# Two scalars by GpSimd's queue, state rows in longer packets, state products copied in halves, and new orders of work

## The chip, the cores and the metric

The kernel runs on one core of one Trainium2 chip. The core has five engines that run side by side, each taking its instructions in its own fixed order: PE (TensorE, matrix products), ACT (ScalarE), DVE (VectorE), POOL (GpSimd) and SP (SyncE). Sixteen DMA engines move data between HBM and the on-chip SBUF; transfers are issued by SP and ACT (hardware queues) and by POOL (the software queue, which can also convert fp32 to fp16 on the way). Matrix products land in PSUM, and only ACT and DVE copy them out. The metric is device time in microseconds (us) of one launch.

## The reference, cut to what matters

```python
B, H, S, Ns, D = 8, 8, 512, 32, 64          # x: (8,8,512,64)  state: (8,8,32,64)
scores = scale * x @ state^T                 # per batch and head, 512 x 32
a      = softmax(scores);   xread = a @ state        # (8,8,512,64)
scores2 = scale * state @ x^T                # 32 x 512
a2     = softmax(scores2);  sread = a2 @ x           # (8,8,32,64)
x = concat([xread, sread], axis=2)           # (8,8,544,64) -> 4352 tokens x 512
h = x @ w_in                                 # 4352 x 2048
g = s * relu(h)**2 + b                       # s and b are two single numbers
out = g @ w_out                              # 4352 x 512
```

## The kernel before, in words

**What it computes, and by which names.** A batch b has 512 x-tokens and 32 state rows for each of 8 heads. `T` is the product of state and x (128 rows: four heads by 32 states, twice), `E` its exponential, `D` the sum over the states, and `a4` the quotient, worked out on ACT as `Ln` and `Exp` of D with a multiplication on DVE. The kernel never forms xread: it multiplies each state by the weights first, `M(b, c)` = state times chunk c of `w_in` (`part_M`, 8 small multiplications, "the state product"), has ACT or DVE copy it from PSUM to SBUF as fp16 (`att_M`), and then multiplies `M` by `a4` (`layer1`, named `h` here; two groups g = 0, 1 of heads are added up). ACT applies relu, DVE squares, and `layer2_first` (batch 0) or `layer2` (all others, with seven products in place of eight from sums of blocks `pd` and of weights `u`) multiplies by `w_out`. s and b come in at the end: `bias_bc` is b times the column sums of `w_out`, and every result is `s * o + bias`.

**How the data come in.** `w_in` is loaded in four chunks `wi[0..3]` (512 columns each), `w_out` in four chunks `wo[0..3]`, and x for each batch as `xn[b]`, all by POOL's queue, which turns fp32 into fp16; each of these lands 512 KB in SBUF. Batch 0's x comes by SP's queue in four parts in fp32 (`x0_load`), and ACT and DVE convert them (`x0_cast`). The states come as `stf[0]` (batch 0, by ACT's queue), `stf[1]` (batches 1 and 2, by POOL's queue) and, later, the rest by SP's queue. `att_st` converts a state and writes it twice side by side (`st16`), PE transposes it, and DVE copies the transposed form to `stT`, which every `T` and `M` reads. POOL's first own instruction is a small copy `gate` that waits for the identity matrix (loaded first on ACT's queue); all of POOL's loads wait behind it. The two single numbers are loaded by SP to four partitions each (`small_load`, L530) and spread to all partitions by a 32x32 transpose on DVE (`spread`, L539).

**What sets the order.** The body calls `op(...)` for each piece of work, which numbers it (0 to 1209). `TURNS` (L17) holds for each engine the list of these numbers in the order in which it runs them, written out by hand. `Plan.order` (L149) walks the lists, keeps a model of times, gives out the buffers (three PSUM pairs `ps`, two single banks `o`, and so on) and, in the first 20 us of its model, puts filler multiplications on `warm` into PE's stream where the model has PE idle. A filler is fixed once the kernel is built: it runs even if PE has other work. A number such as `dma=("sw", MB)` or `lands=` is only an entry of that model.

By the lists, POOL issues: gate, wi0, stf[1], x of batch 1, wi1, wo0, wi2, wo1, wi3, wo2, wo3, x of batch 2. PE runs, in the first 20 us: transposes of x of batch 0, T, D, M(0,0), the transposes of stf[1], h of chunk 0 mixed with the transposes of x of batch 1, M(1,0), M(0,1), T of batch 1, h of chunk 1, and then the first products with wo0.

Of the kernel before, what the change touches and what calls it, by code (L numbers as in the profile page):

```python
# [18 lines left out]
        27 29 25 31 35 33 39 36 40 50 48 80-81 187 84-85 185 53 59 189 92-93 88-89 117 192 118 125-126 121  # L19
        113 122-123 127 119 68 70 114-115 124 116 128 193 120 96 141 129-130 99 237 131-133 225 74 134 142  # L20
        135 145 136 234 137 146 102 147 105 149 148 150-152 161-162 76 108 165-166 240 163 138 111 143
        167-168 164 243 139 222 144 72 62 157 140 158 153 159 56 228 154 160 231 173 155 174 1051 65 330 175
        156 169-171 267 333 258 334 259 268 260-263 269-270 172 176 271 264 272-274 348 351 1056 78 265 345
        354 360 286 277 287-289 694 445 278-281 290-291 282-284 339 357 292 342 293 295-299 454 567 1061
        305-306 300-301 307 302 308 696 576 452 309 315 310 316 311 317 312 318-322 570 572 1066 375-379 448
        689 450 384-387 380 476 388 381-382 467 479 464 389-390 394 482 395 461 391 470 396-397 403 398-401
        473 592 404-405 412 406-407 413-415 408-409 416 410 589 417-419 422 698 692 574 432-436 583 437
        423-424 438 425 439 426-428 586 429 604 601 506 497 507 711 595 498-499 508 598 509 500 510 501-504
        511-512 714 513 516-519 1071 1076 525-526 520-521 527 522-523 528 939 811 529-530 534 531-532
        535-541 544 820 932 935 554-556 545 557-561 546 720 723 619-621 726 622 547-549 705 550-551 623-626  # L30
        717 708 628-630 638-639 631-633 640 634-635 641-642 848 647 643 648-653 644-645 654 845 656-663 1086
        1081 937 941 666-668 676-677 669-670 814 816 818 671-672 678-680 673 954 681 836 741-744 682-683 830
        745-746 957 747 750 748 751-753 833 754-755 760 756 761-763 757 764-766 842 769-770 767 771-775
        778-781 776 782-785 839 788 798-799 789 800 790 801 827 969 963 791 802-805 951 960 1106 792 863 948
        864 793 865 794 866 795 867 1101 868-870 872-878 1091 882 879 883 966 884-888 891-892 1096 889
        893-898 900-906 910 907 911-915 920-921 916-917 1121 1111 984 922 1116 985-986 923 987 924-926
        988-989 927 990 1126 993 991 994-1000 1003-1010 1012-1019 1021-1028 1031-1035 1041 1036 1042
        1037-1038 1043-1048 1143-1150 1152-1159 1162-1169 1171-1178 1180-1187 1190-1197 1200-1207
    """,
    "ACT": """  # L40
        20-21 30 23 37 41 38 42 44 52 45 51 82 86 60 190-191 94 90 194-195 69 197-198 97 100 238 226 235 103
        106 77 109 241 244 223 63 57 229 232 67 331-332 335-336 349 352 79 346 361 355 695 447 446 340 358
# [4 lines left out]
    """,  # L47
    "DVE": """
        24 28 22 26 34 32 6 47 43 49 46 188 83 186 61 7 87 54-55 1057 91 71 95 196 199 98 75 1052 214 101
        239 210 104 215 206 236 107 207 227 110 252 112 218 209 179 177 64 73 245 58 219 242 224 1053 233 66  # L50
        220 230 246 216 253 325 337 183 208 181 247 1058 211 266 248 275 249 347 255 250 256-257 350 356 212
        217 213 285 221 1062 353 254 251 1067 294 341 457 1063 458 303 459 344 369 313 323 1068 363 370 364
        362 359 366 579 371 367 580 365 383 372 581 368 373 392 466 701 402 374 472 1072 484 463 478 469 411
        702 420 481 1077 485 703 475 491 440 585 430 494 594 488 495 492 489 486 588 487 606-608 713 505 597
        514 603 1078 496 493 616 524 940 490 533 1073 542 591 1082 610 936 562 823-824 600 825 944 552 613
        627 1087 617 722 611 945 614 719 636 609 946 728 716 646 615 612 655 707 618 1088 664 1083 942 725
        735 819 710 674 729 684 738 732-733 956 749 730 850 736 739 737 847 758 835 731 768 777 786 734 832
        838 854 740 841 860-861 844 971 959 806 829 855 857 1110 796 851 965 858 852 859 871 962 1105 880
        953 975 856 950 853 972 890 968 1108 899 1103 908 862 976-977 918 1100 981 1098 978 1118 973 1113
        982 928 983 992 979 1125 974 1001 1093 1120 980 1011 1128 1130 1095 1131 1020 1134 1123 1115 1135  # L60
        1029 1137 1140 1136 1138 1132 1141 1039 1049 1151 1160 1133 1142 1170 1139 1179 1188 1198 1208
    """,
    "POOL": """
        8-9 11 16 10 12-15 17-19 329 200 204 202 444 566 180 304 314 276 393 688 810 1060 421 441 182 431
        515 563 324 184 665 178 637 675 1065 1055 759 1070 1080 543 1075 1090 1085 807 685 909 881 919 553
        787 929 797
    """,
    "SP": """
        0-5 327 201 203 328 442 205 443 326 564 338 565 456 1059 687 686 578 460 1064 700 582 1054 704 930
        808-809 931 1079 822 943 1074 826 947 1084 1069 1089 1050 1040 1030 1161 1002 1189 1199 1209  # L70
# [16 lines left out]
class Plan:  # L87
# [60 lines left out]
    def order(self, fill):  # L148
# [3 lines left out]
        dma_free = {"sw": 7.05, "hw": 0.0}  # L152
# [144 lines left out]
def kernel(  # L297
# [88 lines left out]
    few = sb("few", [2], FP32)  # L386
    s32 = sb("s32", [32], FP32)
    b32 = sb("b32", [32], FP32)
    s_bc, b_bc = s32[:, 0:1], b32[:, 0:1]
# [4 lines left out]

    nc.vector.memset(warm, 0.0)
    nc.vector.memset(few, 0.0)
# [9 lines left out]
    for _ in range(4):  # L406
        mm(ob[1], warm[:, 0:P], warm)
    nc.scalar.dma_start(ident16, ident_dr.ap())
    nc.scalar.dma_start(stf[0], st_v[:, 0:NG, :])
# [29 lines left out]
    def x0_load(i):  # L439
        op(  # L440
            {"SP": 0.5},
            lambda e: nc.sync.dma_start(xf_ap(i), x0_v[:, x0_heads(i)]),
            wr=[K(("xf", i))],
            dma=("hw", 0.75),
            lands=(3.6, 4.7, 6.0, 6.5)[i],
        )
# [25 lines left out]
    def wi_load(c):  # L472
        op(
            {"POOL": 0.85},
            lambda e: nc.gpsimd.dma_start(
                out=wi[c],
                in_=moe_w_in.rearrange("(k p) f -> p k f", p=P)[:, :, c * FC : c * FC + FC],
            ),
            rd=[g0],
            wr=[K(("wi", c))],  # L480
            dma=("sw", MB),
        )
# [44 lines left out]
    def small_load(i, src):  # L527
        op(
            {"SP": 0.5},
            lambda e: nc.sync.dma_start(out=few[::32, i : i + 1], in_=src.to_broadcast((4, 1))),  # L530
            wr=[K(("few", i))],
            dma=("hw", 0.1),
            lands=9.8,
        )

    def spread(i, dst, name):
        op(
            {"DVE": 0.12},
            lambda e: nc.vector.transpose(dst, few[:, i : i + 1].to_broadcast((P, 32))),  # L539
            rd=[K(("few", i))],  # L540
            wr=[K((name,))],
        )

    for i in range(4):
        x0_load(i)
    small_load(0, moe_s)
    small_load(1, moe_b)
    spread(0, s32, "s")
    spread(1, b32, "b")
    op(  # L550
# [24 lines left out]
    def att_st(i):  # L575
# [31 lines left out]
        if i == 2:  # L607
# [15 lines left out]
            lambda e: copy(e, stT[:, b0 * NG : b1 * NG], view()[:, 0:n]),  # L623
# [210 lines left out]
    def att_M(b, c, engs=("ACT", "DVE")):  # L834
# [11 lines left out]
        if b == 0 and c < 2:  # L846
            for g in range(NG):
                op(
                    {"ACT": 0.48, "DVE": 0.64},
                    lambda e, g=g: copy(e, T(M[b, c])[:, g], T(u)[:, g]),  # L850
                    rd=[K(u)],
                    wr=[K(M[b, c], g)],
                )
            return
        op(
            {e: {"ACT": 0.92, "DVE": 1.15}[e] for e in engs},
            lambda e: copy(e, T(M[b, c]), T(u)),
            rd=[K(u)],
            wr=[K(M[b, c], g) for g in range(NG)],
        )  # L860

    def att_turn(b, late=False):
        if late:
            after(
                lambda: T(aT[b])[:, 0, 0, 0:2],
# [553 lines left out]
```

## Time and profile before

| | |
|---|---|
| three runs | 207.46, 208.20, 208.53 us; median 208.2 |
| the profiled execution | 208.01 us, of which the profile's span is 206.2 |
| PE busy (fillers included) | 199.3 us, 97% of the span |
| DVE, ACT, POOL busy | 164.3, 109.3 and 38.8 us |
| TensorE clock granted | 1.0 |
| read from HBM, written to it | 17.33 MB, 8.91 MB |

The page is made from one execution. The span runs from the first instruction to the last; the 1.8 us between it and the execution's own time lie around it. Lines of the matrix products all read L335, since one helper issues them, so they are told apart by their operands: `pair<-wi,stT` is M, `pair<-a,M` is h, `o<-wo,g` is layer 2 of batch 0, `o<-warm` or `pair<-warm` is a filler. `stf` in a row stands for either part of the states, `L422` is the helper for copies.

### The profile page before, as it was taken

The numbers are of one execution on the slowest core, as the hardware profiler recorded it, in microseconds if no ns is written. First come the engines' busy times: TensorE is split into PE (matmuls) and PEld (weight loads), VectorE is DVE, ScalarE is ACT, GpSimd is POOL, SyncE is SP. The second block draws the span as 40 slices with busy tenths as digits, with TensorE's granted clock in tenths as the row PEclk, the third lists the DMA queues.
The fourth block names the chain that finished last, engine by engine and source line by source line (L and its number), as shares of the span: only waits on it lengthen the run. The fifth ranks groups of instructions, "written<-read, shape, count | busy, mean of one in ns | idle before, by whom it ended". The sixth has DMA issues, their size and how long they took to land.

```text
span 206.2 us, 4768 instructions
## 1 busy us (share of the span) xinstructions
PE 199.3 (97%) x1989; PEld 134.7 (65%) x1989; DVE 164.3 (80%) x325; ACT 109.3 (53%) x153; POOL 38.8 (19%) x60
## 2 busy tenths in 40 slices
PE   7979999999999999999999999999999999999992
PEld 3744444435666665677577767766776688888881
DVE  2327637989899979899999988997969689859871
ACT  4757786467588879468644473254606634130000
POOL 4832002001020120331301030033070200331000
PEclk9999999999999999999999999999999999999999
DMA  5999999992999992798991470233020200253054
GB/s 173 201 197 204 206 205 179 179 198 16 186 139 195 143 221 41 110 134 154 199 194 60 80 222 13 51 111 118 0 103 3 102 0 2 71 187 105 0 176 131
DMA packets 47285, 25.83 MB, mean 125 GB/s; under 512 B 31616, under 2 KB 45440, under 8 KB 47264
## 3 DMA queue, kind: packets, MB, share of 16 engines
q0 software_dynamic: 13792, 15.34, 38.0%
q1 hardware_dynamic: 33056, 10.10, 26.4%
q8 instruction: 15, 0.25, 0.5%
q10 hardware_dynamic: 416, 0.10, 0.2%
q14 instruction: 6, 0.05, 0.1%
HBM read 17.33 MB, written 8.91 MB: 127 GB/s over the span
## 4 chain that ended last, share of the span: by engine, by line
PE 89%; DMA 7%; DVE 1%; issue 0%; ACT 0%; POOL 0%; DVEq 0%
PE o L335 48%; PE pair L335 41%; DMA wi<-in_moe_w_in_dram 4%; DMA out_dram<-osb 2%; DMA ident<-ident_const 1%; DVE osb L1281 0%; DVE M L422 0%; ACT M L422 0%; DVE osb L1270 0%; DVE aN L906 0%; DVE sr L933 0%; POOL gate L552 0%; DVEq L1270 0%
## 5 line engine op out<-in xcount | busy, mean ns | idle before, releaser
L996 ACT ACTIVATE g<-pair 128x1024 f16<-128x1024 f32 x64 | 63.0, 1023 | 44.5 <-PE pair L335 44.4
L335 PE MATMUL pair<-a,M 128*128 128x512 f16 x256 | 63.3, 379 | 0.1
L335 PEld LDWEIGHTS <-pd 128*128 128x128 f16 x480 | 46.4, 98 | 10.1 <-issue 1.5
L335 PEld LDWEIGHTS <-g 128*128 128x128 f16 x424 | 40.7, 98 | 17.5 <-issue 2.9
L1002 DVE TENSOR_TENSOR g<-g 128x1024 f16<-128x1024 f16 x64 | 42.8, 683 | 2.8 <-ACT g L996 2.8
L335 PE MATMUL o<-u,pd 128*128 128x256 f16 x360 | 44.2, 273 | 0.0
L335 PE MATMUL o<-wo,g 128*128 128x256 f16 (+1 forms) x272 | 42.6, 285 | 0.0
L335 PEld LDWEIGHTS <-M 128*128 128x128 f16 x256 | 24.7, 98 | 22.9 <-DVE M L422 0.6
L1173 POOL DMA_DIRECT2D out_dram<-osb x28 | 18.8, 724 | 103.2 <-DVE osb L1281 54.5
L1270 DVE SCALAR_TENSOR_TENSOR osb<-o,s,bias_bc 128x512 f32<-128x512 f32 (+1 forms) x32 | 22.9, 715 | 7.3 <-PE o L335 5.7
L422 ACT CAST M<-pair 128x1024 f16<-128x1024 f32 (+1 forms) x22 | 20.4, 958 | 7.8 <-PE pair L335 7.8
L1281 DVE SCALAR_TENSOR_TENSOR osb<-o,s,osb 128x512 f32<-128x512 f32 (+1 forms) x24 | 17.2, 716 | 7.6 <-PE o L335 7.4
L1082 DVE TENSOR_TENSOR pd<-g 128x1024 f16<-128x1024 f16 (+1 forms) x32 | 20.7, 651 | 0.1
L335 PE MATMUL o<-wo,pd 128*128 128x256 f16 x120 | 19.0, 273 | 0.0
L335 PE MATMUL o<-u,g 128*128 128x256 f16 x120 | 17.5, 273 | 0.0
L422 DVE CAST M<-pair 128x1024 f16<-128x1024 f32 (+1 forms) x8 | 9.2, 1153 | 4.9 <-PE pair L335 3.8
L1093 DVE TENSOR_TENSOR pd<-g,pd 128x512 f16<-128x512 f16 (+1 forms) x32 | 12.5, 400 | 0.1
L1043 ACT ACTIVATE g<-pair 128x256 f16<-128x256 f32 x16 | 5.3, 385 | 13.0 <-PE pair L335 13.0
L1090 DVE TENSOR_TENSOR pd<-g,pd 128x512 f16<-128x512 f16 (+1 forms) x32 | 12.1, 400 | 0.1
L782 ACT ACTIVATE E<-pair 128x512 f16<-128x512 f32 x16 | 9.5, 600 | 4.7 <-issue 2.3
L335 PE MATMUL pair<-wi,stT 64*32 64x512 f16 x224 | 9.8, 383 | 1.5 <-DMA wi<-in_moe_w_in_dram 1.2
L463 POOL DMA_DIRECT2D xn<-in_x_dram x7 | 6.3, 909 | 25.2 <-ACT g L996 15.1
(70 smaller groups left out, 143.7 us busy)
## 6 DMA issues: line engine op xcount, KB each, us to landing
out_dram<-osb POOLq DMA_DIRECT2D x28, 256.0 KB, 3.2
xn<-in_x_dram POOLq DMA_DIRECT2D x7, 512.0 KB, 8.6
wi<-in_moe_w_in_dram POOLq DMA_DIRECT2D x4, 512.0 KB, 13.2
wo<-in_moe_w_out_dram POOLq DMA_DIRECT2D x4, 512.0 KB, 17.4
u<-in_x_dram SPq DMA_DIRECT2D x4, 256.0 KB, 3.9
out_dram<-osb SPq DMA_DIRECT2D x4, 256.0 KB, 2.7
out_dram<-osb SPq DMA_DIRECT2D x4, 128.0 KB, 2.3
pd<-in_state_dram SPq DMA_DIRECT2D x1, 320.0 KB, 4.0
```

The source lines that it names most:

```text
L335: return nc.tensor.matmul(out, lhsT, rhs, start=start, stop=stop, tile_position=tp, is_transpose=is_transpose, skip_group_check=True,)
L422: (nc.scalar.copy if e == "ACT" else nc.vector.tensor_copy)(dst, src)
L463: lambda e: nc.gpsimd.dma_start(out=T(xn[b]).rearrange("p h c d -> p h (c d)"), in_=x[b].rearrange("h (q c) d -> q h (c d)", q=P),),
L782: nc.scalar.activation(T(E[b])[:, g, :].rearrange("p (m t) -> p m t", m=2), T(u)[:, :, hS * g : hS * g + hS], AF.Exp, scale=scale, accum_o ...
L996: lambda e, u=u, part=part: nc.scalar.activation(part(), T(u), AF.Relu),
L1002: lambda e, part=part: nc.vector.tensor_mul(part(), part(), part()),
L1082: nc.vector.tensor_tensor(view()[:, :, 0:2], blocks(b, j)[:, :, 1:2, :].to_broadcast((P, 2, 2, n)), blocks(b, j)[:, :, 0:4:3, :], ALU.subt ...
L1090: nc.vector.tensor_tensor(view()[:, :, 2], blocks(b, j)[:, :, 3], view()[:, :, 0], ALU.subtract)
L1093: nc.vector.tensor_tensor(view()[:, :, 3], blocks(b, j)[:, :, 2], view()[:, :, 2], ALU.subtract)
L1173: lambda e: eng(e).dma_start(dst, src()),
L1270: lambda e: nc.vector.scalar_tensor_tensor(t_view(u), o_view(bank), s_bc, bias(h), ALU.mult, ALU.add),
L1281: lambda e: nc.vector.scalar_tensor_tensor(t_view(u), o_view(bank), s_bc, t_view(u), ALU.mult, ALU.add),
```

## The change

Five things differ.

- The two numbers are loaded straight to one value in each of the 128 partitions by two transfers on POOL's queue, ahead of everything else on that queue, `gate` included. `few`, its memset, the two loads on SP and the two spreads on DVE are gone.
- The first states are read as they lie in memory: partition q takes r consecutive rows of 64 numbers (r = 2 in `stf[0]`, 512 bytes; r = 4 in `stf[1]`, 1 KB). The right order of columns is made when `stT` is copied out of PSUM, with writes that are r elements apart.
- `stf[1]` moves from POOL's queue to SP's. A one-column copy on DVE from `E` of batch 0, group 1, into `stf[1]` comes before it, so SP waits for that exponential.
- Every state product that was copied whole is copied in two halves, which may go to different engines.
- All five lists are new. There are 1233 pieces in place of 1210.

By the new lists POOL issues: the two numbers, gate, wi0, wi2, wi3, wi1, wo0, x of batch 1, wo1, wo2, wo3, x of batch 2. PE runs at the start: transposes of x of batch 0 (all four), T, D, M(0,0), then h of chunk 0, M(0,2), h of chunk 2, M(0,3), h of chunk 3, M(0,1), the rest of chunk 3, h of chunk 1, and the first products with wo0, and only then the transposes of stf[1] and of x of batch 1. ACT runs the two Ln and the two Exp of batch 0 before the two halves of M(0,0). In the old list 50 places of PE's list pass from one kind of product to another (plain, four-part rows, four-part columns), in the new one 52.

```diff
-        27 29 25 31 35 33 39 36 40 50 48 80-81 187 84-85 185 53 59 189 92-93 88-89 117 192 118 125-126 121
+        22 24 20 26 28 30-31 34-35 47 87-88 83 65 84 99 74 102 108 56 105 91-92 95-96 116 120 117 124
...
-        20-21 30 23 37 41 38 42 44 52 45 51 82 86 60 190-191 94 90 194-195 69 197-198 97 100 238 226 235 103
+        16 18 27 32-33 36 39 37 40 48-49 89 67 85 100 76 103 58 109 106 93 97 194 193 69 200-201 197-198
...
-        8-9 11 16 10 12-15 17-19 329 200 204 202 444 566 180 304 314 276 393 688 810 1060 421 441 182 431
+        4-5 8 10 6-7 11 9 12-14 203 332 205 207 447 573 185 307 327 187 183 699 1083 279 317 825 444 522 424
...
-        dma_free = {"sw": 7.05, "hw": 0.0}
+        dma_free = {"sw": 6.95, "hw": 0.0}
...
-    few = sb("few", [2], FP32)
-    s32 = sb("s32", [32], FP32)
-    b32 = sb("b32", [32], FP32)
-    s_bc, b_bc = s32[:, 0:1], b32[:, 0:1]
+    s_bc = sb("s_bc", [1], FP32)
+    b_bc = sb("b_bc", [1], FP32)
...
+    def st_near(b0, b1):
+        rows = state[b0:b1].rearrange("b h j d -> (b h j) d")
+        return rows.rearrange("(q r) d -> q r d", q=P)
+
     nc.vector.memset(warm, 0.0)
-    nc.vector.memset(few, 0.0)
...
+    nc.gpsimd.dma_start(out=s_bc, in_=moe_s.to_broadcast((P, 1)))
+    nc.gpsimd.dma_start(out=b_bc, in_=moe_b.to_broadcast((P, 1)))
     nc.scalar.dma_start(ident16, ident_dr.ap())
-    nc.scalar.dma_start(stf[0], st_v[:, 0:NG, :])
+    nc.scalar.dma_start(stf[0], st_near(0, 1))
...
-            lands=(3.6, 4.7, 6.0, 6.5)[i],
+            lands=(3.75, 4.7, 5.95, 6.25)[i],
...
-            dma=("sw", MB),
+            dma=("sw", MB + 0.4 * (c == 2)),
...
-    def small_load(i, src):
-        op(
-            {"SP": 0.5},
-            lambda e: nc.sync.dma_start(out=few[::32, i : i + 1], in_=src.to_broadcast((4, 1))),
...
-    def spread(i, dst, name):
-        op(
-            {"DVE": 0.12},
-            lambda e: nc.vector.transpose(dst, few[:, i : i + 1].to_broadcast((P, 32))),
...
-    op(
-        {"POOL": 0.9},
-        lambda e: nc.gpsimd.dma_start(out=stf[1], in_=st_v[:, NG : NS * NG, :]),
-        rd=[g0],
-        wr=[K(("stf", 1))],
-        dma=("sw", 0.45),
-    )
...
-            lambda e: copy(e, stT[:, b0 * NG : b1 * NG], view()[:, 0:n]),
+            lambda e: copy(
+                e,
+                stT[:, b0 * NG : b1 * NG].rearrange("p n q -> p (n q)").rearrange("p (q r) -> p r q", r=n),
+                view()[:, 0:n],
+            ),
...
-        if b == 0 and c < 2:
-            for g in range(NG):
-                op(
-                    {"ACT": 0.48, "DVE": 0.64},
-                    lambda e, g=g: copy(e, T(M[b, c])[:, g], T(u)[:, g]),
-                    rd=[K(u)],
-                    wr=[K(M[b, c], g)],
-                )
-            return
-        op(
-            {e: {"ACT": 0.92, "DVE": 1.15}[e] for e in engs},
-            lambda e: copy(e, T(M[b, c]), T(u)),
-            rd=[K(u)],
-            wr=[K(M[b, c], g) for g in range(NG)],
-        )
+        for g in range(NG):
+            op(
+                {"ACT": 0.48, "DVE": 0.64},
+                lambda e, g=g: copy(e, T(M[b, c])[:, g], T(u)[:, g]),
+                rd=[K(u)],
+                wr=[K(M[b, c], g)],
+            )
...
+    op(
+        {"DVE": 0.08},
+        lambda e: nc.vector.tensor_copy(stf[1][:, 0, 0:2], T(E[0])[:, 1, 0:2]),
+        rd=[K(E[0], 1)],
+        wr=[K(("stf", 1))],
+    )
+    op(
+        {"SP": 0.5},
+        lambda e: nc.sync.dma_start(out=stf[1], in_=st_near(1, NS)),
+        wr=[K(("stf", 1))],
+        dma=("hw", 2.6),
+        lands=13.2,
+    )
     att_st(1)
```

More of the change, by code (lines that the diff above doesn't have):

```diff
@@ L18 @@
     "PE": """
-        27 29 25 31 35 33 39 36 40 50 48 80-81 187 84-85 185 53 59 189 92-93 88-89 117 192 118 125-126 121
[L20 to L38, printed above, removed]
+        22 24 20 26 28 30-31 34-35 47 87-88 83 65 84 99 74 102 108 56 105 91-92 95-96 116 120 117 124
@@ new lines @@
+        128-129 121 45 130 125 118 188 190 126 122 119 127 68 192 131 140 123 136-137 144 138 196 139 145
+        132-134 152 141 135 195 153 142 148 154 143 149-150 77 111 155 151 164 168-169 246 114 165 170 166
+        171 167 237 240 50 146 243 59 147 228 156 160 225 157 71 53 158-159 161 231 234 162-163 176-177 333
+        62 1074 178 172 179 270-271 337 336 261 173 272 174 273-275 262 276 263-266 175 267 277 345 351 348
+        268 1079 354 280 342 281-283 289 80 709 448 290-292 284 357 285-287 293-294 460 706 295-296 363
@@ new lines @@
+        298-300 360 301-303 308 304-305 309 586 577 574 310-315 318-320 454 451 1084 321-323 378 324 379 457
+        580 700 380 325 381-383 474 387-389 486 468 384 471 390 385 477 483 397 391 398-399 703 1089 400-401
+        392-394 489 402-403 406-410 404 411 480 412-413 415-422 603 425 600 426 583 712 427 435-437 428
+        438-440 429-430 441-442 431 594 432 597 504-506 609 507-508 615 513 509 514 510 515 511 516 612 606
+        517-518 729 519-520 523-525 726 532-533 526-530 534-539 826 1094 1099 551 541-548 552-554 951 954
@@ new lines @@
+        960 555 561-563 556-557 564-566 558 567 732 568 630-631 741 735 639 632 640 633-635 641 636-637 642
+        738 723 643-646 649-650 838 832 963 651-654 658 655-656 659-661 720 662 667 663 668-670 664-665 864
+        671-674 867 677-678 687 679-680 1109 1104 835 829 957 688 681 689-691 682 692 846 683 693 852 684
+        694 858 756 861 765 757 766 758 767 759 768 760-763 980 769-771 775 772 855 776 784 777 785-786 778
+        787 779 788-789 780-782 849 790 793-794 791 795-800 803 977 813-818 804 971 983 819 986 989 805-806
@@ L39 @@
+        820 807-808 1114 809 974 882-884 810 885-889 992 891-893 901 1124 902 894-896 903 897-898 904 1119
+        905-908 910-916 919 917 920-926 929-930 1129 931 939-940 932 941 933 942-943 1139 944-945 934-936
+        1144 946 1134 1149 1007-1013 1016 1014 1017-1023 1026-1030 1035 1031 1036 1032 1037 1033 1038-1042
+        1044-1051 1054-1059 1064-1065 1060-1061 1066-1071 1166-1173 1175-1182 1185-1192 1194-1201 1203-1210
+        1213-1220 1223-1230
     """,
     "ACT": """
-        20-21 30 23 37 41 38 42 44 52 45 51 82 86 60 190-191 94 90 194-195 69 197-198 97 100 238 226 235 103
@@ L42 @@
-        106 77 109 241 244 223 63 57 229 232 67 331-332 335-336 349 352 79 346 361 355 695 447 446 340 358
[4 rows of a table removed]
+        16 18 27 32-33 36 39 37 40 48-49 89 67 85 100 76 103 58 109 106 93 97 194 193 69 200-201 197-198
+        78-79 112 247 238 51 241 244 61 229 226 54 73 55 232 235 334-335 63 338-339 346 352 349 355 343 82
+        711 449-450 358 81 462 461 708 364 707 361 587 576 588 575 579 456 452 455 459 458 702 701 475
+        581-582 487 469 472 478 484 704 490 481 604 585 713 584 714 601 595 598 610 616 613 727 730 607 828
@@ L47 @@
+        827 953 955 952 956 733 742 736 739 724 834 833 965 840 865 721 868 830 837 831 959 958 836 847 859
+        862 856 850 853 978 981 972 984 987 1115 975 1117 993 990 1120 1125 1122 1132 1130 1142 1127 1140
+        1150 1135 1147 1152 1137 1145
     """,
     "DVE": """
-        24 28 22 26 34 32 6 47 43 49 46 188 83 186 61 7 87 54-55 1057 91 71 95 196 199 98 75 1052 214 101
-        239 210 104 215 206 236 107 207 227 110 252 112 218 209 179 177 64 73 245 58 219 242 224 1053 233 66
-        220 230 246 216 253 325 337 183 208 181 247 1058 211 266 248 275 249 347 255 250 256-257 350 356 212
@@ L52 @@
[L52 to L61, printed above, removed]
[4 rows of a table added]
@@ new lines @@
+        362 326 369 366 375 370 373 590 488 367 386 591-592 479 376 476 371 395 368 485 377 473 1091 405 470
+        374 492 414 705 716 423 717 495 491 496 718 443 482 433 602 498 596 493 1095 494 501 512 599 502 497
+        611 499 1100 605 500 521 621-622 614 531 540 1096 503 728 608 1101 549 731 618 961 617 747 559 627
+        569 1110 619 624 628 842 629 1105 962 638 843 625 844 743 647 839 725 964 657 623 967 626 666 620
+        675 968 737 722 1111 1106 969 869 740 744 734 750 685 748 695 751 753 745 848 764 863 754 773 866
@@ L62 @@
+        746 752 783 792 749 801 851 860 755 854 982 857 870-871 973 979 821 988 873 876 985 874 811 879 890
[4 rows of a table added]
     """,
     "POOL": """
-        8-9 11 16 10 12-15 17-19 329 200 204 202 444 566 180 304 314 276 393 688 810 1060 421 441 182 431
-        515 563 324 184 665 178 637 675 1065 1055 759 1070 1080 543 1075 1090 1085 807 685 909 881 919 553
-        787 929 797
+        4-5 8 10 6-7 11 9 12-14 203 332 205 207 447 573 185 307 327 187 183 699 1083 279 317 825 444 522 424
+        550 560 396 676 1078 648 1093 181 774 1108 434 1098 802 1103 1088 696 686 1113 812 928 570 948 900
@@ L67 @@
+        822 938
     """,
     "SP": """
-        0-5 327 201 203 328 442 205 443 326 564 338 565 456 1059 687 686 578 460 1064 700 582 1054 704 930
-        808-809 931 1079 822 943 1074 826 947 1084 1069 1089 1050 1040 1030 1161 1002 1189 1199 1209
+        0-3 43 331 204 330 206 208 445-446 329 341 571 463 572 697-698 467 589 1077 593 715 1082 823-824 719
+        950 949 1087 841 966 845 1092 1102 970 1097 1107 1112 1053 1063 1184 1025 1073 1212 1222 1232
     """,
@@ L525, in st_load @@
         )
-    def small_load(i, src):
-        op(
-            {"SP": 0.5},
-            lambda e: nc.sync.dma_start(out=few[::32, i : i + 1], in_=src.to_broadcast((4, 1))),
-            wr=[K(("few", i))],
-            dma=("hw", 0.1),
-            lands=9.8,
-        )
-    def spread(i, dst, name):
-        op(
-            {"DVE": 0.12},
-            lambda e: nc.vector.transpose(dst, few[:, i : i + 1].to_broadcast((P, 32))),
-            rd=[K(("few", i))],
-            wr=[K((name,))],
-        )
     for i in range(4):
         x0_load(i)
[L546 to L549, printed above, removed]
     op(
@@ L845, in att_M @@
             return
-        if b == 0 and c < 2:
-            for g in range(NG):
-                op(
-                    {"ACT": 0.48, "DVE": 0.64},
-                    lambda e, g=g: copy(e, T(M[b, c])[:, g], T(u)[:, g]),
-                    rd=[K(u)],
-                    wr=[K(M[b, c], g)],
-                )
-            return
-        op(
-            {e: {"ACT": 0.92, "DVE": 1.15}[e] for e in engs},
-            lambda e: copy(e, T(M[b, c]), T(u)),
-            rd=[K(u)],
-            wr=[K(M[b, c], g) for g in range(NG)],
-        )
+        for g in range(NG):
[5 more added lines that the diff above has]
+            )
     def att_turn(b, late=False):
```

12 rows, old and new, of the table TURNS are left out of this document.

## The prediction

> **What bounds the kernel now.** First the page's busy times, then the same times by stage.
>
> ```profile
> span 206.2 us, 4768 instructions
> PE 199.3 (97%) x1989; PEld 134.7 (65%) x1989; DVE 164.3 (80%) x325; ACT 109.3 (53%) x153; POOL 38.8 (19%) x60
> ```
>
> ```profile
> 0.00:11.72 11.72, 9.25 (x79) 5.98 (x79) 3.00 (x16) 6.66 (x12) 6.71 (x13) 1.00 0.91 186
> 11.72:18.64 6.92, 6.89 (x90) 4.18 (x89) 3.52 (x8) 4.26 (x7) 3.37 (x4) 1.00 1.26 203
> 18.64:50.00 31.36, 31.24 (x253) 12.96 (x252) 23.33 (x43) 22.22 (x31) 2.00 (x4) 1.00 1.07 173
> 50.00:100.00 50.00, 49.73 (x562) 32.83 (x561) 45.73 (x86) 37.71 (x49) 9.08 (x12) 1.00 0.94 146
> 100.00:150.00 50.00, 50.00 (x570) 35.55 (x568) 46.22 (x82) 24.85 (x31) 7.21 (x11) 1.00 0.42 100
> ```
>
> The columns are PE, PEld, DVE, ACT, POOL, the clock, the DMA share and GB/s. From 18.64 us on PE has no hole worth naming (0.27 us in 50 to 100, none in 100 to 150), so nothing can be won there; the end comes earlier only if PE reaches that stage with more done. Before 18.64, busy is not useful: PE's timeline shows fillers.
>
> ```profile
> 10.23 0.27 PE L335 MATMUL pair<-warm 128*128 128x256 f16 x1
> 11.72 0.41 PE L335 MATMUL pair<-wi,stT 64*32 64x512 f16 x8 [1.21 <-DMA wi<-in_moe_w_in_dram]
> 12.06 0.94 PE L335 MATMUL o<-warm 128*128 128x256 f16 x7
> ...
> 13.06 0.82 PE L335 MATMUL o<-warm 128*128 128x256 f16 x6
> 13.81 1.04 PE L335 MATMUL pair<-a,M 128*128 128x512 f16 x4
> ...
> 17.08 0.50 PE L335 MATMUL pair<-warm 128*128 128x256 f16 x3
> ...
> 18.07 0.72 PE L335 MATMUL pair<-warm 128*128 128x256 f16 x5
> ```
>
> The chain of waits says what comes ahead of 11.72: the identity's load, the gate, and one transfer of 8.27 us.
>
> ```profile
> 3.29 0.12 POOL gate L552
> 3.41 8.27 DMA wi<-in_moe_w_in_dram
> ```
>
> Last, the DMA view from 5.5 to 9.6 us, and from 9.6 to 11.7 us:
>
> ```profile
> q0 software_dynamic: 641, 0.67, 102.3%
> ...
> q0 software_dynamic: 659, 0.35, 131.8%
> ```
>
> By 9.6 us the software queue had moved 0.67 MB, more than the 0.52 MB of the first wi, which yet landed only at 11.68. The trace's records of single packets show why: fifteen DMA engines end their share (32 packets of 1 KB, one each 79 ns) between 8.5 and 9.6 us; one engine starts at 7.49, its first packet takes 1008 ns in place of 98, later ones 535 and 339, and it ends at 11.62. It stays behind: the next big transfers land at 14.85, 17.45 and 20.0, 2.55 us apart.
>
> **The change part by part.**
>
> *The two numbers.* Two more POOL issues at 0.76 to 0.91 us (POOL's load rows), 1.5 to 1.8 us. POOL idles 2.84 us ahead of the gate, so from about 0.75 they end by 2.6 and the gate still waits for the identity until 3.23: nothing on the path. If that cover failed, every POOL load behind the gate would move, one for one. Gone are SP's 0.67 and 0.54 us (nothing follows on SP for 20 us), and on DVE a memset of 0.06 and two spreads of 0.20, in DVE's waits or beside a busy PE: nothing. What 128 packets of 4 bytes do on the DMA engines, no row shows. From below: 4-byte packets took 9 to 22 ns in the records, sixteen per engine some 0.3 us. From above: one more first packet of 1.0 us. They reach the engines while x of batch 0 flows (2 to 6.6 us).
>
> *The first wi's landing* is the term that decides. The small loads are now the first on the software queue. Bounds: 0 (the late engine stays late) and −2.0 us (it ends with the others at 9.6; also below by as much, +2.2, if its three stalls come once more for the small loads). I take the stalls of 1008 and 535 ns for those of a queue being started, (1.01 − 0.10) + (0.54 − 0.10) = 1.35 us, and let the small loads take them; the 339 ns stay. The first wi then lands at 10.35.
>
> *State rows.* The same bytes; `stf[0]` landed at 5.0, two microseconds ahead of T. The copies to stT (0.28 and 0.43 us) write with gaps: between the same time and twice; +0.2 at most is hidden, since T waits for the last part of x. `stf[1]` on SP: its wait is for the exponential of group 1, about 9.6; nothing else is queued on SP. It lands 3.8 to 7.8 us later (the rows of stf), 13.4 to 17.4. Behind its cast DVE queues the copy of M(0,1), needed at 18.5: hidden. Its 128 KB still go between the first and second big transfer: the spacing there was 3.17 in place of 2.55; I keep 0.45 to 0.6.
>
> *Halves.* ACT copies 19 whole products (1.016 us) and 6 halves before, 48 halves after; consecutive halves start 0.49 apart (12.19, 12.68), though one lasts 0.588. So ACT gains between 42 × 0.49 − 19.3 = 1.3 and 42 × 0.588 − 19.3 = 5.4 us. DVE goes from 7 whole (1.219) and 6 halves (0.684) to 16 halves, −1.7 us. ACT idles 44.4 us waiting for PE in the relu group alone: nothing.
>
> *The new order*, counted from the first wi's landing, W. Before: from 11.72 to 18.64 there are 6.92 us, of which 21 fillers at 0.109 are 2.3; useful are three state products and T (0.87), 20 transposes (1.12), 8 products h of 0.216 (1.73), and four turns between kinds of product at 0.1 (an estimate from the steps between such rows), together 4.1; the rest are waits. So 2.8 us are lost after W. After: the second, third and fourth wi land at W+3.0, +5.55 and +8.1, wo0 at +10.65. PE does all of h of batch 0 first (32 × 0.216 = 6.9), four state products (0.86) and eight turns (0.8), 8.6 us. The last wi gates M(0,1) at W+8.1; then 0.4 us for it with its turn, 0.3 for its copy, five steps of 0.43 and 0.3 for a PSUM pair still under relu: wo0's first product at W+11.25. Lost are 11.25 − 8.6 = 2.65. The order is worth −0.15; the list's two more turns (52 against 50) cost 0.2. Nothing, then: x of batch 1 is no longer early, but three wi in a row feed PE no faster than 2.55 us each. The softmax of batch 0 (ACT: two Ln, two Exp ahead of the copies) ends near 12.4 by the rows' lengths; PE needs 5.5 us between there and W+8.1 = 18.45, so 0.5 is spare.
>
> *Sum*, against the profiled execution: 208.01 − 1.35 − 0.15 + 0.2 = 206.7. That execution lay 0.2 under the median of the runs, so 206.9 for a median.
>
> The Trainium skill, "DMA: Bandwidth & Descriptors", section "Latency and other measured facts", has a rule against this: engines 7 and 15 are usually the slower ones, and its best guess (called uncertain) is contention at the ports that serve the software queue's descriptor rings. The trace has one late engine and no number for it. By that rule the lateness belongs to an engine and not to a start, and the time is rival B's.
>
> **The rivals.**
>
> *B, the late engine stays as late.* For it: only one of sixteen is late, while all start the same queue; its stalls fall into 7.5 to 9.7, while POOL issues without pause (3.4 to 9.8), and POOL will do that again. Against: no such stall later, not while POOL issues wo2 and wo3. Then 208.2 − 0.15 + 0.2 = 208.2.
>
> *C, slower: the small loads add to the lateness.* The late engine reads three transfers' first descriptors instead of one's; each costs a first packet, 0.9 us, or all three stalls, 2.2. Everything after W moves with it. From W = 11.8 on it is slower than before: 208.2 + 0.9 to 2.2 = 209.1 to 210.4, say 209.6. Against: POOL has them out 0.8 us before the gate.
>
> *D, slower: the new lists stall past 20 us*, where the old ones did not. DVE is at 91 and 92% there. Two places in which a half stands behind a relu on ACT (1.02 us each), with PE out of banks, take 2.0 us: 206.9 + 2.0 = 208.9, or 210.2 from B. It decides, against A's gain, from two such places. Against: DVE has 1.7 us less.
>
> **How the numbers follow.** No change and 0.5% (1.04 us) are about what this kernel's runs can tell apart. A (as summed) 0.42, its own range 206.2 (the whole 2.0 gone) to 207.4 (one stall more left); B 0.28; C 0.15; D 0.15. Faster than 207.16: nearly nine tenths of A and a little of B, 0.39. Slower than 209.24: two thirds of C and half of D's upper part, 0.18; within, 0.43. The range goes from A's low end, 206.2, into C, 209.4.
>
> **What would show it.** Right: the first wi lands near 10.4 (critical transfer 7 us from the gate), the later ones 2.55 apart; fillers or waits of 2.5 to 3 us between there and the first product with wo0 near 21.5; gate still at 3.29; no PE hole past 25 us. B shows as a landing at 11.5 or later, C as one past 12 or a gate past 3.4, D as idle PE between 25 and 185 us. Wrong altogether: x of batch 0 delayed by the small packets beyond 0.5 us, so that h starts past 13.

## The result

The changed kernel takes 213.82 us (median; 213.3 to 214.42) against 207.83 for the kernel before in the same series: the ratio is 1.029, 95% interval 1.024 to 1.034. The forecast was 206.9 with a range of 206.2 to 209.4, so it was wrong, and on the wrong side. The profiled execution took 213.66 us with a span of 211.9, 5.7 us more than before. Of all executions behind the times below one, of the second experiment (212.78 us), was in a slower state of the chip and is left out.

The page's first lines, and the busy times by stage (the same columns as before: PE, PEld, DVE, ACT, POOL, clock, DMA share, GB/s):

```profile
span 211.9 us, 4775 instructions
PE 201.6 (95%) x1985; PEld 135.0 (64%) x1985; DVE 165.1 (78%) x327; ACT 112.3 (53%) x175; POOL 39.1 (18%) x61
```

```profile
0.00:11.72 11.72, 7.09 (x53) 4.56 (x54) 3.52 (x15) 3.00 (x4) 7.78 (x15) 1.00 0.65 157
11.72:18.64 6.92, 6.92 (x50) 3.83 (x50) 1.53 (x4) 4.87 (x11) 1.62 (x2) 0.75 1.23 213
18.64:50.00 31.36, 30.14 (x237) 12.71 (x236) 20.09 (x36) 21.16 (x31) 1.36 (x4) 1.00 1.12 181
50.00:100.00 50.00, 49.76 (x614) 31.25 (x599) 47.71 (x90) 37.56 (x61) 8.74 (x12) 1.00 0.89 141
100.00:150.00 50.00, 50.00 (x566) 35.10 (x564) 45.43 (x84) 29.51 (x44) 7.87 (x11) 1.00 0.48 100
```

From 50 us on nothing is lost (0.24 us of idle PE in 50 to 100, 0.27 before). All of the loss lies ahead of it, and most ahead of 18.64 (M(0,0) starts 3.9 of the 5.7 us later): in the first stage the DMA share fell from 0.91 to 0.65, and ACT did 3.0 us of work in place of 6.7. The chain of waits of the first 12 us no longer runs through the first wi. Where the gate and a wi of 8.27 us stood, it has the last of the four loads of batch 0's x (`u<-in_x_dram`), on SP's hardware queue:

```profile
2.27 8.12 DMA u<-in_x_dram
10.39 0.02 issue
10.41 0.63 ACT xn L428
```

In the kernel before, the four loads took 3.2 to 4.5 us, and the last was there by about 6.7. PE's timeline shows what hangs on it: the last two groups of transposes of batch 0, the sums D, and then M(0,0), which came at 11.72 before. (The helper that issues the products is at L338 in this kernel, the one for copies at L428 or L429.)

```profile
9.84 0.40 PE L338 MATMUL pair<-ident,xn 128*128 128x128 f16 x4 [2.59 <-DVE xn L428]
...
11.09 0.40 PE L338 MATMUL pair<-ident,xn 128*128 128x128 f16 x4 [0.84 <-ACT xn L428]
...
13.78 0.63 PE L338 MATMUL o<-E,bones 128*128 128x512 f16 x1
14.21 1.49 PE L338 MATMUL pair<-warm 128*128 128x256 f16 x6
15.63 0.41 PE L338 MATMUL pair<-wi,stT 64*32 64x512 f16 x8
```

What held up the loads of x is seen in the DMA view of 4.5 to 7.5 us, in 40 slices (tenths busy; GB/s), first of the kernel before, then of the kernel after:

```profile
DMA  9897888999999999986676999989999999899999
...
q0 software_dynamic: 258, 0.26, 63.0%
q1 hardware_dynamic: 484, 0.45, 44.6%
```

```profile
DMA  1012112232544554332111011120112432644555
...
q1 hardware_dynamic: 304, 0.30, 29.2%
q0 software_dynamic: 40, 0.00, 1.0%
```

In the kernel after the engines move 100 GB/s in the mean of these 3 us in place of 237, with work queued on both queues (four wi were issued between 2.81 and 5.89). The trace's records of single packets show 32 packets of 32 bytes from 4.27 to 9.06 us, 16 for each number, that is one per engine by their count (the records do not number the engines): the 256 four-byte reads of s and b. The two loads themselves land 5.7 and 7.4 us after they are issued:

```profile
s_bc<-in_moe_s_dram POOLq DMA_DIRECT2D x1, 0.5 KB, 5.7
b_bc<-in_moe_b_dram POOLq DMA_DIRECT2D x1, 0.5 KB, 7.4
```

### The profile page after: what moved, and what is told of

The parts are those of the page before. It is cut to its first block, busy times and chain, and to the rows that moved or that the text cites. A ratio compares the mean times of both kernels' runs of the same rounds, so it can differ in the third digit from the quotient of the medians.

```text
span 211.9 us, 4775 instructions
## 1 busy us (share of the span) xinstructions
PE 201.6 (95%) x1985; PEld 135.0 (64%) x1985; DVE 165.1 (78%) x327; ACT 112.3 (53%) x175; POOL 39.1 (18%) x61
## 4 chain that ended last, share of the span: by engine, by line
PE 89%; DMA 4%; DVE 2%; ACT 2%; SPq 1%; issue 0%; DVEq 0%
PE o L338 48%; PE pair L338 40%; DMA u<-in_x_dram 4%; DVE M L428 1%; ACT M L428 1%; SPq L448 1%; DVE stT L428 1%; ACT g L970 0%; ACT xn L428 0%; DVE g L976 0%; DVE osb L1244 0%; DVEq L428 0%
## 5 line engine op out<-in xcount | busy, mean ns | idle before, releaser
L970 ACT ACTIVATE g<-pair 128x1024 f16<-128x1024 f32 x64 | 63.7, 1028 | 39.1 <-PE pair L338 38.7
L338 PE MATMUL pair<-a,M 128*128 128x512 f16 x256 | 64.1, 379 | 1.2 <-ACT M L428 0.7
L338 PEld LDWEIGHTS <-pd 128*128 128x128 f16 x480 | 46.3, 98 | 11.7 <-issue 2.0
L338 PEld LDWEIGHTS <-g 128*128 128x128 f16 x424 | 40.8, 98 | 16.6 <-issue 1.9
L338 PE MATMUL o<-u,pd 128*128 128x256 f16 x360 | 44.2, 273 | 0.0
L338 PE MATMUL o<-wo,g 128*128 128x256 f16 (+1 forms) x272 | 41.1, 285 | 0.0
L338 PEld LDWEIGHTS <-M 128*128 128x128 f16 x256 | 24.5, 98 | 23.4 <-DVE M L428 1.5
L1244 DVE SCALAR_TENSOR_TENSOR osb<-o,s_bc,bias_bc 128x512 f32<-128x512 f32 (+1 forms) x32 | 22.9, 715 | 8.8 <-PE o L338 8.3
L428 ACT CAST M<-pair 128x512 f16<-128x512 f32 x43 | 23.3, 594 | 7.4 <-PE pair L338 5.9
L1255 DVE SCALAR_TENSOR_TENSOR osb<-o,s_bc,osb 128x512 f32<-128x512 f32 (+1 forms) x24 | 17.2, 716 | 4.6 <-PE o L338 4.4
L338 PE MATMUL o<-wo,pd 128*128 128x256 f16 x120 | 18.9, 273 | 0.0
L338 PE MATMUL o<-u,g 128*128 128x256 f16 x120 | 17.7, 273 | 0.0
L428 DVE CAST M<-pair 128x512 f16<-128x512 f32 x13 | 8.9, 688 | 7.1 <-ACT M L428 3.5
L1067 DVE TENSOR_TENSOR pd<-g,pd 128x512 f16<-128x512 f16 (+1 forms) x32 | 12.9, 409 | 0.0
L1064 DVE TENSOR_TENSOR pd<-g,pd 128x512 f16<-128x512 f16 (+1 forms) x32 | 12.5, 401 | 0.1
L924 POOL COPY srd<-srdT 128x128 f16<-128x128 f16 x8 | 9.1, 1187 | 10.2 <-DMA srdT<-sr 10.2
```

What stands on the lines that cost most here:

```text
L338: return nc.tensor.matmul(out, lhsT, rhs, start=start, stop=stop, tile_position=tp, is_transpose=is_transpose, skip_group_check=True,)
L428: (nc.scalar.copy if e == "ACT" else nc.vector.tensor_copy)(dst, src)
L924: lambda e: nc.gpsimd.tensor_copy(srd[:, :, :, b], srdT[:, b]),
L970: lambda e, u=u, part=part: nc.scalar.activation(part(), T(u), AF.Relu),
L1064: nc.vector.tensor_tensor(view()[:, :, 2], blocks(b, j)[:, :, 3], view()[:, :, 0], ALU.subtract)
L1067: nc.vector.tensor_tensor(view()[:, :, 3], blocks(b, j)[:, :, 2], view()[:, :, 2], ALU.subtract)
```

## The experiments

Each time stands beside the kernel before on the same chip; the ratio is the measure.

### Undoing the scalars, or making that change alone

The first edit takes the two numbers out of the changed kernel's POOL queue and loads them as before: SP reads each into four partitions behind x, and DVE spreads them.

```diff
-    nc.gpsimd.dma_start(out=s_bc, in_=moe_s.to_broadcast((P, 1)))
-    nc.gpsimd.dma_start(out=b_bc, in_=moe_b.to_broadcast((P, 1)))
...
+            if i == 3:
+                for k, src in enumerate((moe_s, moe_b)):
+                    nc.sync.dma_start(out=few[::32, k : k + 1], in_=src.to_broadcast((4, 1)))
...
+            if b == 1:
+                for k, dst in enumerate((s32, b32)):
+                    nc.vector.transpose(dst, few[:, k : k + 1].to_broadcast((P, 32)))
```

> The kernel after, with the two numbers loaded as before (four partitions each, by SP's queue behind the four loads of x, then two spreads on DVE). Theory 1, the 256 four-byte reads of the two numbers hold up the DMA engines: between 4.6 and 9 us the engines carry traffic again, the last part of x of batch 0 lands near 6.5 in place of 10.4, and the time is 207.5 to 209. Theory 2, the small loads matter little and the new lists, the halves and the copy with gaps cost the time: 212 to 214.

Measured: 209.07 us, ratio 1.006 (1.002 to 1.010). So 4.75 of the 6.0 us go with the scalars (4.8 by the ratios); the rest, +0.6%, stays. In the DMA view of 4.5 to 7.5 us the traffic is back:

```profile
DMA  9999999999869968679678975899989899999799
```

The second edit does that part alone in the kernel before: the two POOL loads first, SP's two loads and the spreads left out.

> The kernel before, with only the loads of the two numbers as in the kernel after (all 128 partitions, first on POOL's queue; SP's two loads and the two spreads left out). Theory 1: the gap in the DMA traffic comes with them, x of batch 0 lands some 3.5 us late, and the time is 211 to 213. Theory 2: 207.5 to 208.5.

Measured: 211.31 us (the middle one of 209.52, 211.31 and 211.81), ratio 1.014 (1.005 to 1.022); the last packet of x starts at 9.33 us in place of 6.34, and the same hole stands in the DMA view of 4.5 to 7.5 us:

```profile
DMA  3344576655331030011100000000000112123547
```

Theory 1 holds in both directions, though with three executions so far apart the size is loose here.

### What in the small loads does it

The same two loads, at the same place and of the same form, but of 128 different numbers:

```diff
-    nc.gpsimd.dma_start(out=s_bc, in_=moe_s.to_broadcast((P, 1)))
+    nc.gpsimd.dma_start(out=s_bc, in_=x[0, 0, 0:2, :].rearrange("s (d o) -> (s d) o", o=1))
...
```

`b_bc` is changed in the same way, to the next 128 numbers of x.

> The kernel after, with the two loads at the same place and of the same form, but each reading 128 different numbers of x instead of one number 128 times (s and b are then wrong, the rest is the same). Theory 1a, it is the one address that is read by all engines at once: no gap in the traffic, x lands by 7 us, 207.5 to 209.5. Theory 1b, it is the size of the pieces, or that they come first on the software queue: 213 to 214.5, as the kernel after.

Measured: 208.86 us, ratio 1.005 (1.002 to 1.008), level with the loads on SP. The packets are the same 32 of 32 bytes, but they take 1.5 us (4.05 to 5.52) in place of 4.8, and x's last packet starts at 6.6 in place of 9.9. In the DMA view of 4.5 to 7.5 us:

```profile
DMA  3347989999899977589699997798999999999999
```

So it is neither the size of the pieces nor their place on the software queue, but what they read: one number 128 times. The edit changes two things at once, though, the repeat and the tensor: that the two numbers lie in a slow place would fit as well, and 128 reads of one number of x were not tried. The eight reads of the old form are too few to tell.

The same two loads from SP's hardware queue, behind x:

```diff
-    nc.gpsimd.dma_start(out=s_bc, in_=moe_s.to_broadcast((P, 1)))
-    nc.gpsimd.dma_start(out=b_bc, in_=moe_b.to_broadcast((P, 1)))
...
+            if i == 3:
+                nc.sync.dma_start(out=s_bc, in_=moe_s.to_broadcast((P, 1)))
+                nc.sync.dma_start(out=b_bc, in_=moe_b.to_broadcast((P, 1)))
```

> The kernel after, with the same two loads to 128 partitions issued by SP behind the four loads of x, in place of POOL. Theory 1a: the traffic stalls too, but behind x and against the first wi: x of batch 0 lands by 7 us, the first wi 3 us later than in the kernel before (14 to 15), 210 to 213. Theory 1b with the software queue as the cause: 207.5 to 209.5.

Measured: 212.29 us (two executions, 211.3 and 213.28), ratio 1.021 (1.010 to 1.031). x lands in time, and the hold-up falls on what comes next, the first wi. From about 5.8 to 7.3 us the traffic is at nothing, and PE waits:

```profile
13.22 0.41 PE L338 MATMUL pair<-wi,stT 64*32 64x512 f16 x8 [2.98 <-DMA wi<-in_moe_w_in_dram]
```

So the software queue is not the cause either.

One number read 128 times first on POOL's queue, the other on SP by four partitions:

```diff
-    nc.gpsimd.dma_start(out=b_bc, in_=moe_b.to_broadcast((P, 1)))
...
+            if i == 3:
+                nc.sync.dma_start(out=few[::32, 0:1], in_=moe_b.to_broadcast((4, 1)))
```

> The kernel after with one number read 128 times on POOL's queue and the other by SP to four partitions as before. If the hold-up grows with the number of reads of one address: x of batch 0 lands some 1.8 us late in place of 3.7, and the time is half-way, 211 to 212. If one such load is hidden under the loads of x: 209 to 209.5.

Measured: 209.89 us, ratio 1.009 (1.006 to 1.013). Its 16 packets span 2.5 us (3.6 to 6.1) where 32 took 4.8: about 19 ns for each read of the same address in both (2.5 us / 128, 4.8 us / 256). x's last packet starts at 7.4, 1.8 us later than with both loads on SP (5.65), as was expected of a hold-up that grows with the reads. The time does not grow in the same way: one load costs 0.8 us over none (the intervals overlap, so it may be nothing), two cost 4.75. Neither end of what was expected for the time fits; most of the first load's hold-up is hidden.

The same two loads on POOL's queue, issued behind x of batch 2:

```diff
-    nc.gpsimd.dma_start(out=s_bc, in_=moe_s.to_broadcast((P, 1)))
-    nc.gpsimd.dma_start(out=b_bc, in_=moe_b.to_broadcast((P, 1)))
...
+            if b == 2:
+                nc.gpsimd.dma_start(out=s_bc, in_=moe_s.to_broadcast((P, 1)))
+                nc.gpsimd.dma_start(out=b_bc, in_=moe_b.to_broadcast((P, 1)))
```

> The kernel after with the same two loads on POOL's queue, but issued behind x of batch 2 instead of first. The reads of one address then fall at 30 to 36 us behind the weights; x of batch 0 and the first wi land as with the loads on SP (6.5 and 11). If the hold-up costs only where something early waits for the engines: 208.8 to 209.8, as with the loads on SP. If s arrives too late for the first result (needed at 38.9 us) or x of batch 2 is held up: 210 to 213, with PE idle between 35 and 50 us.

Measured: 209.82 us, ratio 1.010 (1.006 to 1.013), just above what was expected; its interval overlaps the one with the loads on SP (1.002 to 1.010), and the profiled span is 207.5, against 207.4 there. A hole in the traffic stands at 32 to 34 us. In the DMA view of 28 to 45 us, first of this kernel, then with the loads on SP:

```profile
DMA  9999999993320595999999999999999999998998
...
DMA  9999999999774187999999999999999999997999
```

Part of this hole is there without the loads too, so it cannot all be put down to them. And the packets go by faster than before: all 32 span 2.4 us (31.87 to 34.27), and 24 of them 0.3 us. So 19 ns for a read is what the early loads took, and no fixed price. PE is idle only 0.09 us in 40 to 50. The loads cost where something early waits for the engines; behind the weights they cost between nothing and some 0.8 us.

### The other 0.6%

With the scalars as before, PE's and ACT's rows of the next stage show what is left. PE's timeline, then ACT's, then DVE's:

```profile
14.34 0.41 PE L338 MATMUL pair<-wi,stT 64*32 64x512 f16 x8
...
16.26 0.82 PE L338 MATMUL pair<-a,M 128*128 128x512 f16 x3 [0.23 <-ACT M L429]
...
26.86 0.61 PE L338 MATMUL pair<-ident,xn 128*128 128x128 f16 x8 [0.30 <-DVE stT L429]
```

```profile
15.62 0.58 ACT L429 CAST M<-pair 128x512 f16<-128x512 f32 x1 [0.58 <-DVE M L429]
```

```profile
14.89 0.69 DVE L429 CAST M<-pair 128x512 f16<-128x512 f32 x1 [2.40 <-PE pair L338]
...
25.51 1.30 DVE L429 COPY stT<-pair 128x512 f16<-128x512 f16 x1 [0.25 <-PE pair L338]
```

The two halves of M(0,2), on DVE and ACT, do not run side by side: ACT waits for DVE, and both take 1.31 us from 14.89 to 16.20. And the copy of stT with gaps takes 1.30 us; without gaps the kernel before needed 0.43.

The first edit puts the products of batch 0 with chunks 1, 2 and 3 into two single PSUM banks in place of one PSUM pair:

```diff
-    APART = {(1, 0), (1, 1), (2, 0), (2, 1)}
+    APART = {(0, 1), (0, 2), (0, 3), (1, 0), (1, 1), (2, 0), (2, 1)}
```

> The kernel after with the two numbers loaded as before, and the first three state products of batch 0 after M(0,0) (chunks 1, 2 and 3) put into two single PSUM banks each in place of one PSUM pair. Theory H, the two halves run one after the other on DVE and ACT because both lie in one PSUM tile: the halves then overlap (starts within 0.1 us), the first product with wo0 starts 0.6 to 1.2 us earlier than 23.57, and the time falls by 0.5 to 1.1 us, to 207.9 to 208.6. Rival, the order of the two is set by the buffer M that both write: they stay 0.7 us apart and the time stays at 209.

Measured: 207.73 us, ratio 0.999 (0.997 to 1.002). The halves now overlap (DVE 14.15, ACT 14.28, chunk 2; both still write one buffer M), the first product with wo0 starts at 21.65 in place of 23.57, of which 0.66 come from an earlier M(0,0) (10.63 against 11.29), and PE does not wait for M. So the order of the two halves came from the common PSUM tile:

```profile
14.15 0.69 DVE L429 CAST M<-o 128x512 f16<-128x512 f32 x1 [2.24 <-PE o L338]
14.28 0.58 ACT L429 CAST M<-o 128x512 f16<-128x512 f32 x1
```

The order is a wait on a semaphore that the program carries; whether the two banks of one tile could be read at once without it was not tried.

The second edit, made without the first, reads the states in the old layout:

```diff
-    nc.scalar.dma_start(stf[0], st_near(0, 1))
+    nc.scalar.dma_start(stf[0], st_v[:, 0:NG, :])
...
-            lambda e: nc.sync.dma_start(out=stf[1], in_=st_near(1, NS)),
+            lambda e: nc.sync.dma_start(out=stf[1], in_=st_v[:, NG : NS * NG, :]),
...
-                stT[:, b0 * NG : b1 * NG].rearrange("p n q -> p (n q)").rearrange("p (q r) -> p r q", r=n),
-                view()[:, 0:n],
+            lambda e: copy(e, stT[:, b0 * NG : b1 * NG], view()[:, 0:n]),
```

> The kernel after with the two numbers loaded as before, and the states read in the old layout (256-byte packets, stT copied without gaps; stf[1] still on SP). Theory S, the copy with gaps (1.30 us for 128x512) holds up the transposes of x of batch 1 behind it: the copy takes 0.43 us, PE's wait of 0.30 for stT goes, the time falls by 0.2 to 0.5 us, to 208.6 to 208.9. Rival, the wait is taken over by the next one: 209.0 as without it.

Measured: 208.6 us, ratio 1.002 (1.000 to 1.005). The copy takes 0.42 us and PE's wait for stT is gone; the intervals of this and of the kernel without the edit (1.002 to 1.010) overlap, so its own worth (0.4% by the ratios) is not settled, and may be nothing.

Both edits together:

> Both edits together. H and S: 207.4 to 208.3, level with the kernel before. If neither matters, 209, and what is left over the kernel before lies in the new orders.

Measured: 207.55 us, ratio 0.999 (0.996 to 1.001). With the scalars, the PSUM tile and the layout undone, what remains of the change (the new orders, stf[1] on SP, the other halves) is level with the kernel before. None of these versions is measurably faster than it.

### The halves themselves

Where both halves go to one engine, one instruction copies the whole product again:

```diff
+            if not one:
+                copy(e, T(M[b, c])[:, g], T(u)[:, g])
+            elif place[k] < place[n + n + 1 - k]:
+                copy(e, T(M[b, c]), T(u))
```

> The kernel after with the two numbers loaded as before, and every state product whose two halves go to the same engine copied in one instruction again (at the place of its first half; chunks 0 and 1 of batch 0 and the products shared by two engines keep their halves). If the halves cost ACT's time for the relus past 30 us: faster than 209.07 by 0.3 us or more. If they are hidden, as forecast: within 0.3 us of 209.07, since 17 pairs at most at 0.98 against 1.02 us change ACT by less than 3 us of 100 idle.

> The same edit on top of the two numbers as before, single banks for three products of batch 0, and the old layout of the states (207.55 without it). Hidden halves: 207.3 to 207.9, level with the kernel before. If halves past 30 us help or harm by themselves: a change of more than 0.3 us, of the same sign as in the other run.

Measured: 209.85 us (ratio 1.010, 1.007 to 1.014) and 207.76 us (1.000, 0.997 to 1.003). The first lies 0.8 us above the time without the edit, outside the 0.3 us that were expected, the second within. Both intervals overlap those without the edit (1.002 to 1.010 and 0.996 to 1.001), though both lie on the slower side; PE's idle time in 50 to 100 us goes from 0.24 to 0.60 us in each. So no cost of the halves on one engine is seen; whether they save something these runs do not settle.

## Why the prediction was wrong, point by point

- **The DMA engines' price for the small packets** is the step that failed. It was bounded by sixteen 4-byte packets at 9 to 22 ns per engine (0.3 us) and one late first packet (1.0 us). Neither row is of a number that is read 128 times. Measured: the 256 reads came as 32 packets of 32 bytes, took 4.8 us in the kernel after, some 19 ns each if they ran one after another, and held the engines up meanwhile. A bound from the nearest row was no bound, since no row had what is peculiar about this load, the repeat. The 4-partition form hid it: 8 reads.
- **Where it falls.** The sum let the small loads act only on the first wi, the next on their queue. They acted on x of batch 0, on another queue, since the engines are shared: +3.6 us at its last packet. The closing sentence of the forecast named this ("x of batch 0 delayed by the small packets beyond 0.5 us"), but it had no price and no chance. Rival C had the right part, the small loads, with the wrong victim and less than half the size (0.9 to 2.2 us against 4.75).
- **POOL's issues are covered** by its wait ahead of the gate: right. They took 0.69 and 0.56 us, and the gate ran at 2.69, earlier than before.
- **The first wi lands earlier, −1.35.** Wrong for the change, where it landed at about 12.6. Whether small loads take a queue's starting stalls stays open: with 128 different addresses at the same place it landed at about 9.8, the earliest of all profiles here, but in the versions with the loads on SP it varied from 10.2 to 11.5. The reading of the stalls was also too narrow: the packet of 1008 ns was not the only long one, since 21 other packets of 1 KB on that queue took 160 to 530 ns ahead of 8.2 us in the kernel before. (The prediction's times of single packets, 7.49 to 11.62 and the 8.5 to 9.6, are 0.24 us too late by the clock of the views; its durations are right.) And even 9.8 paid little: with it M(0,0) came 0.55 us earlier than in the kernel with the loads on SP, the first product with wo0 0.54, and the times are level. ACT's softmax and the fillers of 1.5 us behind M(0,0) stood next in line. The forecast set it at 0.5 us spare and did not follow it.
- **The new order, near nothing from W.** Wrong by 1 us as the change stands: from M(0,0) to the first product with wo0 it takes 12.3 us, with the loads on POOL (15.63 to 27.92) and on SP alike, where 11.25 was worked out from W. Only in single banks, which the forecast did not have, is it 11.0. The step that failed is "0.3 for its copy" and its like for the other chunks: a pair of halves on two engines takes 1.3 us. The rows were in the profile of before: M(0,1) on ACT at 18.00 and on DVE at 18.61, with DVE's wait for ACT; a product in single banks had both at 43.7.
- **The copy of stT with gaps.** "Between the same time and twice" failed: 0.43 to 1.30 us at steps of four elements, 0.28 to 0.44 at steps of two. The copy for batch 0 (steps of two) was hidden as said; the other, at 25.51, made PE wait 0.3 us.
- **stf[1] on SP, halves on one engine, stages past 50 us:** hidden, as said (PE idle 0.24 us in 50 to 100, none in 100 to 150). Rival D did not come about: with the loads on SP, PE waits 0.8 us between 20 and 30 us, for the halves of M(0,1) (0.47) and for the copy of stT (0.30); no half that stands behind a relu is among them.
- **The Trainium skill's rule** on slower engines ("DMA: Bandwidth & Descriptors", "Latency and other measured facts") was set up as rival B. No run here decides it: the traces do not number the engines. Another rule of that page of the Trainium skill bears on the change and was not weighed: its "Rules for kernel authors" warn that an outermost dimension of c below 16, such as a leading broadcast of c copies, confines a load to at most c engines, and advise 128 partitions outermost. Followed here, with one number as the source, each load came in 16 packets, as many as there are engines, and by these runs the form of four copies was 4.75 us better.

The clock granted to PE was 0.5 from 12.3 to 15.7 us in the kernel after, and from 10.3 to 13.7 in the kernel before with the new loads; no other profile here has it before 200 us. Why it fell is open: with the loads from SP's queue PE waited 2.98 us and its profile shows the full clock. What it cost was not measured apart. From the end of the last transposes of batch 0's x to M(0,0) it took 4.1 us in the kernel after (11.49 to 15.63) and 3.0 with the loads on SP (8.33 to 11.29), so up to some 1.2 us of the 4.75 may be the clock's. And of the three executions of the kernel before with the new loads, the one at full clock took 209.52 us, the two at 0.99 in the mean 211.31 and 211.81. So the hold-up is the start of the loss, and the lower clock may be a part of its price.

## What to carry to other kernels

A load that reads one address many times is not small because its bytes are few: count the reads of the address, reckon with up to 19 ns for each in a row on all engines, and look at what else those engines carry just then. Read one number into a few partitions and spread it on the chip (209.07 us in place of 213.82 here), or load it where nothing early waits (209.82). And before a copy is split over two engines, look whether halves of one PSUM tile have ever overlapped in the trace.

## What was not expected of the hardware

Reading one number of HBM 128 times slows the DMA engines far beyond its bytes. At the start of the kernel it took about 19 ns a read, as if the reads ran one behind another (128 reads in 2.5 us, 256 in 4.8), and meanwhile the other transfers on these engines, on either queue, got 100 GB/s in the mean of 4.5 to 7.5 us in place of 237, and none for over 1 us when the loads came from SP's queue. Later in the kernel 256 such reads took 2.4 us. With 128 neighbouring but different addresses the same packets took a third (1.5 us for 256 reads). Whether it is the repeated address or the place of the two numbers, and why it is slow, was not tested.
